# Inputs laid out by numpy in tile order, the second half of d descending, the transforms over d folded about the middle between two columns, one transfer per tile

## The chip, the cores and the metric

The kernel runs on one core of one Trainium2 chip. The metric is the device time of one execution in microseconds (us), and the number to be predicted is the median of the runs of the changed kernel. Rearranging arrays with numpy ahead of the launch, or the result behind it, is on the host and is not in that time.

## The reference

The shapes are S = 2048 tokens, D = 576 features, F = 4608 hidden units, all in 32-bit floats.

```python
xn = (x - mean(x)) / sqrt(var(x) + 1e-5)          # over D, x: [1, 2048, 576]
a  = irfft2(rfft2(xn, axes=(-2, -1)) * (w_r + 1j * w_i), s=(S, D))
b  = (sigmoid(xn @ w_gate) * (xn @ w_up)) @ w_down   # [576, 4608] twice, [4608, 576]
out = x + a + b
```

## The kernel before

**Sizes.** P = 128 partitions. The tokens make NT = 16 tiles of 128, in PAIRS = 2 pairs of 8 tiles; a pair is two chunks of CW = 512 tokens. F makes NF = 36 blocks of 128, and a block of one pair is a *unit*: 72 units in all. HD = 288 is half of D, and 288 rows are worked on as two pieces of 128 and a remainder of REM = 32. A tile of x holds the 128 tokens that leave two neighbouring remainders modulo N2 = 32, so its rows lie 32 rows apart in DRAM, and `load_x` (L340) brings it in with two transfers of 64 rows of 576 floats.

**The gated layer.** Products that need 32-bit accuracy are made of a rounded high part and a low part of each operand. ACT makes the high part with a copy, DVE the low part with a subtraction. One product (`prod`, L648) is 7 matmuls of 128x512. Units 0 and 1 of a pair are `plain` with 8 products per unit. All later ones (`unit`) use 7 products of sums and differences of the halves of xn and of the weights. The banks A, B and E of PSUM, written pA, pB and pE, collect them; between products ACT copies bank A to B, reads B into v (L712) and makes the sigmoid g (L716). `X` holds the transposed tokens with their parts: `fill` transposes x tiles on PE into px (L438, L439), ACT copies them into X (L442) and DVE makes their low part (L444). xa holds the normalised tokens, mv their moments (DVE, L351 and L352), rs their scales (L358 to L360).

**Weights.** In pair 0 every unit's weights are prepared. `load_raw` (L218, L219) brings the four 288x128 quarters of a block of w_gate and w_up into a raw tile of 128 x 4 x 3 x 128 floats: for each quarter one transfer of 2 x 128 rows, and one that puts the 32 remaining rows into the tile four times. That is 8 transfers per unit. `make_w` then makes the sums and parts (ACT L231; DVE L233, L255 to L258) and stores the result into DRAM (`wsp`, L271); the plain units do so in `make_p` (store at L262). Pair 1 reads the stored parts back (L278). w_down goes the same way: `load_d` (L285), `parts_d` (ACT L290, DVE L292), and, for the blocks whose second layer is done in 7 products, `make_t` (sums wt, then wth on ACT L312 and wtl on DVE).

**The second layer and the spectral branch.** `down` (matmuls po L755, added at L759) multiplies by w_down; in pair 1 `seven` (ps, L846, L856) does most of it. Also in pair 1 the transform runs "aside", a step between two products: `phase1b` for 16 tiles (fold of d about column 288 on DVE, transposes pf, the transform over d pd at L491, one over 64 of the tokens' indices pa at L503, stored to sc1), `phase2` for 16 steps (another transform pb L532, multiplication by w_r and w_i, L539 to L541, and back, pc L549), and `phase3` for 16 tiles (py L576, pz, the inverse over d pe L605, sums into the output tile L609 to L612, out). The fold takes e(d) = x(d) + x(576-d) and o(d) = x(d) - x(576-d) for d = 0 to 288: 289 columns, the second operand read backwards, with one padded column; so a remainder there has FR = 33 rows. KOF is the order in which the frequencies stand in the tiles: 1 to 256, 0, 257 to 288.

**What sets the order of the work.** DMA issues are mostly on SP, some at the start and the end on ACT. All engines work through their instructions in order. The kernel is written with Tile: the Python program calls the parts in turn, and a scheduler then sets each engine's order from the program's order and its own costs, except where `tc.keep_in_program_order` holds an instruction. So the diff alone does not tell the order. The program's own order at the start is this (L889 to L892):

```python
    for i in range(TPP):
        new_acc(0, i)
        if i in (TPC - 1, TPC + 1):
            load_raw(i // TPC)
```

Eight x tiles are asked for, with the raw tiles of units 0 and 1 after the fourth and the sixth of them.

## Time and profile before

| what | number |
|---|---|
| runs, us | 1441.50, 1441.35, 1441.07 |
| median, us | 1441.35 |
| span of the profiled execution, us | 1439.6 |
| DVE's costliest group, L759, 168 instructions | 126.0 us |
| DMA moved | 338.86 MB in 184747 packets, mean 235 GB/s |
| queue q1 (SP's transfers) | 72.2% of 16 engines' span |

How to read it: the profile shows one execution, whose span is 1.75 us shorter than the median of the timed runs. Each engine's busy time and number of instructions, the chain of waits and the stretches with idle time are shown where the prediction uses them. In a row of the timeline, the columns are the start in us, the length in us, the engine, its line of the program, the operation, output <- input, and the number of instructions; in brackets stands the idle time of the engine before it and what ended it. In a row of the windows stand the stretch, its length, the busy time of PE, PEld (PE's weight loads), DVE, ACT and POOL with their instruction counts, the granted TensorE clock (1.00 is full), the share of the DMA engines' time that was busy, and GB/s. A row of the groups holds line, engine, operation, shapes, count, the busy time and the mean in ns, and idle time before them.

### The profile page before, as it was taken

To read this page: it belongs to the slowest core of one execution; us is meant where nothing else is said; L and a number is where in the kernel's file an instruction comes from. 1 tells how busy PE (TensorE), PEld (TensorE's weight loads), DVE (VectorE), ACT (ScalarE), POOL (GpSimd) and SP (SyncE) were. 2 spreads that over 40 slices of the span, in tenths; PEclk is the share of its full clock that TensorE was granted. 3 is DMA by queue.
4 is the path that set the end of the run, shared out by engine and by line. 5 is a ranking of instruction groups with operands and counts; after the bars stand their busy time and mean duration, and the time that the engine had idled before them with its cause. 6 is when DMAs were issued, how large, how long until landed. Compare 5 with 4: busy or idle time off the path is not lost.

```text
span 1439.6 us, 21954 instructions
## 1 busy us (share of the span) xinstructions
PE 1425.9 (99%) x8073; PEld 1254.3 (87%) x8073; DVE 1093.5 (76%) x1798; ACT 652.3 (45%) x1122; POOL 4.8 (0%) x21
## 2 busy tenths in 40 slices
PE   8999999999999999999999999999999999999998
PEld 5888888888888888888888888888888889899997
DVE  6988788888888888756366787767888877766784
ACT  5644444444444444444345444444555534443432
POOL 0000000000000000000000000000000000000000
PEclk8999999999999999999999999999999999999999
DMA  6588788787777778664667767668998887776642
GB/s 209 207 277 294 263 295 285 254 274 258 263 261 255 262 254 277 230 231 167 226 210 203 212 197 214 196 198 275 271 275 272 267 276 246 228 224 198 204 126 83
DMA packets 184747, 338.86 MB, mean 235 GB/s; under 512 B 15808, under 2 KB 108480, under 8 KB 179776
## 3 DMA queue, kind: packets, MB, share of 16 engines
q1 hardware_dynamic: 183712, 336.15, 72.2%
q8 instruction: 64, 1.05, 0.3%
q10 hardware_dynamic: 928, 1.31, 0.3%
q14 instruction: 43, 0.35, 0.1%
HBM read 201.28 MB, written 136.12 MB: 234 GB/s over the span
## 4 chain that ended last, share of the span: by engine, by line
PE 94%; DVE 2%; DMA 1%; SPq 1%; ACT 1%; issue 1%; DVEq 0%; ACTq 0%
PE pB L648 23%; PE po L755 18%; PE pE L648 16%; PE pA L648 15%; PE ps L846 12%; PE pd L491 2%; PE pe L605 2%; PE pc L549 1%; PE py L576 1%; PE pa L503 1%; PE pb L532 1%; DMA raw<-in_B_w_up 1%; PE pf L475 1%; PE pz L588 1%; SPq L218 0%
## 5 line engine op out<-in xcount | busy, mean ns | idle before, releaser
L648 PE MATMUL pB<-X,w 128*128 128x512 f32 x1484 | 383.0, 395 | 1.9 <-ACT w L231 1.5
L648 PEld LDWEIGHTS pB<-X,w 128*128 128x128 f32 x1484 | 267.8, 188 | 51.8 <-ACT w L231 1.9
L648 PE MATMUL pE<-X,w 128*128 128x512 f32 x1064 | 272.5, 392 | 0.2 <-DVE y L713 0.2
L648 PE MATMUL pA<-X,w 128*128 128x512 f32 x1008 | 259.4, 395 | 0.3 <-DVE X L444 0.2
L648 PEld LDWEIGHTS pE<-X,w 128*128 128x128 f32 x1064 | 192.7, 188 | 34.6 <-DVE y L713 0.7
L648 PEld LDWEIGHTS pA<-X,w 128*128 128x128 f32 x1008 | 184.5, 190 | 33.9 <-DVE X L444 0.7
L755 PE MATMUL po<-wd,hh 128*128 128x288 f32 x1216 | 210.9, 295 | 0.0
L846 PE MATMUL ps<-wf,hs 128*128 128x288 f32 x1260 | 206.0, 296 | 0.3 <-issue 0.3
L846 PEld LDWEIGHTS ps<-wf,hs 128*128 128x128 f32 x1260 | 189.3, 188 | 19.4 <-DVE qs L856 1.9
L755 PEld LDWEIGHTS po<-wd,hh 128*128 128x128 f32 x1216 | 184.4, 188 | 11.2
L759 DVE TENSOR_TENSOR acc<-acc,po 128x576 f32<-128x576 f32 x168 | 126.0, 750 | 77.9 <-PE po L755 76.8
L231 ACT ACTIVATE w<-raw 128x768 fp32r<-128x768 f32 (+1 forms) x106 | 100.8, 952 | 115.6 <-PE pE L648 47.5
L755 PE MATMUL po<-wd,hl 128*128 128x288 f32 x608 | 128.9, 293 | 0.0
L856 DVE TENSOR_TENSOR qs<-qs,ps 128x576 f32<-128x576 f32 x112 | 84.1, 751 | 28.6 <-PE ps L846 27.9
L755 PEld LDWEIGHTS po<-wd,hl 128*128 128x128 f32 x608 | 98.7, 189 | 0.0
L733 DVE TENSOR_TENSOR y<-y,g 128x1024 f32<-128x1024 f32 x67 | 82.0, 1223 | 4.4 <-DVE y L732 0.5
L233 DVE TENSOR_TENSOR w<-raw,w 128x512 fp32r<-128x512 f32 (+1 forms) x106 | 82.0, 773 | 4.3 <-ACT w L231 3.3
L856 DVE TENSOR_TENSOR acc<-acc,ps 128x576 f32<-128x576 f32 x90 | 67.5, 750 | 22.9 <-PE ps L846 22.5
L716 ACT ACTIVATE g<-pB 128x512 f32<-128x512 f32 x68 | 40.7, 598 | 93.6 <-PE pB L648 93.5
L782 ACT ACTIVATE hs<-y 128x512 fp32r<-128x512 f32 x105 | 64.5, 628 | 34.3 <-DVE y L820 10.3
L732 DVE TENSOR_TENSOR y<-v,pE 128x512 f32<-128x512 f32 x67 | 45.9, 686 | 39.4 <-PE pE L648 39.3
L713 DVE TENSOR_TENSOR y<-v,pE 128x512 f32<-128x512 f32 x68 | 46.7, 687 | 33.7 <-ACT v L712 33.0
(166 smaller groups left out, 1678.8 us busy)
## 6 DMA issues: line engine op xcount, KB each, us to landing
w<-wsp SPq DMA_DIRECT2D x246, 320.0 KB
wsp<-w SPq DMA_DIRECT2D x34, 2240.0 KB
wdsp<-wd SPq DMA_DIRECT2D x36, 576.0 KB
wf<-tsp SPq DMA_DIRECT2D x60, 288.0 KB
wf<-wdsp SPq DMA_DIRECT2D x45, 288.0 KB
std<-in_B_w_down SPq DMA_DIRECT2D x36, 288.0 KB
raw<-in_B_w_gate SPq DMA_DIRECT2D x72, 128.0 KB
raw<-in_B_w_up SPq DMA_DIRECT2D x72, 128.0 KB
```

Of the source, the lines that this page charges most:

```text
L231: placed(nc.scalar.activation(o[:, :, :3, :], src, AF.Copy))
L233: placed(nc.vector.tensor_tensor(o[:, :, 3:, :], src[:, :, :KT, :], f32(o[:, :, :KT, :]), op=OP.subtract))
L648: nc.tensor.matmul(bank, w[:, sw, :], X[:, x, sx, :], start=start and j == 0, stop=stop and j == len(STEPS) - 1, skip_group_check=skip)
L713: nc.vector.tensor_tensor(y[:, 1], v[:, 1], bank["E"], op=OP.add)
L716: nc.scalar.activation(g[:, 1], bank["B"], AF.Sigmoid)
L732: nc.vector.tensor_tensor(y[:, 0], v[:, 0], bank["E"], op=OP.add)
L733: nc.vector.tensor_tensor(y, y, g, op=OP.mult)
L755: nc.tensor.matmul(pd[:, b, :HD], h[i], w[k][b], start=g == 0 and n == 0, stop=g == G - 1 and n == 2)
L759: nc.vector.tensor_tensor(a, a, pd[:, :, :HD], op=OP.add)
L782: nc.scalar.activation(hs[:, 0], src, AF.Copy)
L846: nc.tensor.matmul(pd[:, i, :HD], h[:, a, m], w[:, b], start=q == 0, stop=q == 2)
L856: nc.vector.tensor_tensor(o, o, pd[:, :, :HD], op=OP.add)
```

## The change

The host lays the inputs out in the order in which the tiles read them: x in tile order, w_gate and w_up as one array `w` with a raw tile of 128 x 1536 floats per block, the remainder rows repeated in it, w_r and w_i as one array `ri` with a tile per step of phase 2, frequencies already in the order KOF and both halves of the partitions filled. Of x, of the rows of w_gate and w_up and of the columns of w_down, the second half of d stands in descending order (COLS). The result is put back into its natural order on the host.

- A tile of x, a raw tile, a tile of ri, and an output tile of pair 0 are one transfer each; the raw tiles of units 0 and 1 are two halves. The last output tiles keep two transfers, on SP and ACT.
- The fold is about 287.5, between two columns: d with 575 - d. Its operands are the two halves as they lie, 288 columns each, none read backwards; POOL's fill of the padded column goes. The remainder of the fold has 32 rows in place of 33, and the inverse transform's matmuls (pe) write 288 columns in place of 290, as do od and the sums behind them.
- In phase 2 the two products with w_r and w_i are one instruction each over 578 columns; before they were three each (512, 2 and 64 columns).

```diff
+COLS = np.concatenate([np.arange(HD), np.arange(HD, D)[::-1]])
+ROWS = np.arange(S).reshape(N1, N2).T.ravel()
...
+    ks = np.concatenate([np.arange(KT * P), np.tile(np.arange(KT * P, HD), 4)])
+    w = np.stack([w_gate[COLS], w_up[COLS]]).reshape(2, 2, HD, NF, P)[:, :, ks]
+    w = w[[1, 1, 0, 0], [0, 1, 1, 0]].reshape(4, KT + 1, P, NF, P).transpose(3, 2, 0, 1, 4)
+    v = np.stack([w_r, w_i])[:, :, KOF].reshape(2, N1, N2 // 2, 2, KD).transpose(2, 1, 0, 3, 4)
...
     def load_raw(f):
-        cols = slice(f * P, (f + 1) * P)
         RAW[f] = raw = R["pool"].tile([P, 4, 3, P], F32, tag="raw", name=f"raw{f}", bufs=2)
-        for src, blks in ((w_gate, (3, 2)), (w_up, (0, 1))):
-            v = src.rearrange("(h r) f -> h r f", h=2)
-            for h, b in enumerate(blks):
-                nc.sync.dma_start(raw[:, b, :KT, :], v[h, :KT * P, cols].rearrange("(k p) f -> p k f", p=P))
-                nc.sync.dma_start(raw[:, b, KT, :], v[h:h + 1, KT * P:, cols].to_broadcast([4, REM, P]))
+        n = (KT + 1) * P
+        for b in ((2, 4), (0, 2)) if f < G else ((0, 4),):
+            nc.sync.dma_start(raw[:, slice(*b)].rearrange("p b k f -> p (b k f)"), w_in[f, :, b[0] * n:b[1] * n])
...
-        nc.sync.dma_start(STD[j][:, g], w_down[f * P:(f + 1) * P, :])
+        nc.sync.dma_start(STD[j][:, g], w_down[f])
...
-    def load_x(dst, t, eng=None):
-        for i, r in enumerate(rows(x, t)):
-            (eng or nc.sync).dma_start(dst[i * N1:(i + 1) * N1, :D], r)
+    def load_x(dst, t):
+        nc.sync.dma_start(dst, x[t])
...
-        xb = pool.tile([P, D + 2], F32, tag="xb", name=f"xb{t}", bufs=2)
+        xb = pool.tile([P, D], F32, tag="xb", name=f"xb{t}", bufs=2)
-        nc.gpsimd.memset(xb[:, D:], 0.0)
-            nc.vector.tensor_tensor(eo[:, e, :HD + 1], xb[:, :HD + 1], xb[:, HD:D + 1][:, ::-1], op=op)
-        rp = pool.tile([P, 2, 3, FR], F32R, tag="rp", name=f"rp{t}")
+            nc.vector.tensor_tensor(eo[:, e], xb[:, :HD], xb[:, HD:], op=op)
+        rp = pool.tile([P, 2, 3, REM], F32R, tag="rp", name=f"rp{t}")
...
-        for nm, src in (("wr", w_r), ("wi", w_i)):
-            w = pool.tile([P, 2, KD], F32, tag=nm, name=f"{nm}{i}", bufs=2)
-            v = src.rearrange("(k kl) n -> k (kl n)", kl=N2)[:, kl * KD:(kl + 2) * KD]
-            for a in range(2):
-                nc.sync.dma_start(w[a * N1:(a + 1) * N1].rearrange("p j n -> p (j n)"), v)
+        w = pool.tile([P, 2, 2, KD], F32, tag="ri", name=f"ri{i}", bufs=2)
+        nc.sync.dma_start(w.rearrange("p a j n -> p (a j n)"), ri[i])
...
-        for q, k in ((slice(0, 256), slice(1, 257)), (slice(256, 257), slice(0, 1)), (slice(257, KD), slice(257, KD))):
-            nc.vector.tensor_tensor(z[:, :, q], wr[:, :, k], pb[:, :, q], op=OP.mult)
-            nc.vector.tensor_tensor(t2[:, :, q], wi[:, :, k], sw[:, :, q], op=OP.mult)
+        nc.vector.tensor_tensor(z, wr, pb[:, :, :KD], op=OP.mult)
+        nc.vector.tensor_tensor(t2, wi, sw, op=OP.mult)
...
-                nc.tensor.matmul(pe[:, e, :NQ], l, r, start=n == 0, stop=n == len(steps) - 1)
+                nc.tensor.matmul(pe[:, e, :HD], l, r, start=n == 0, stop=n == len(steps) - 1)
-        lo, up = a[:, :HD + 1], a[:, HD + 1:][:, ::-1]
+        lo, up = a[:, :HD], a[:, HD:]
```

In the orders below a row is an engine's line, operation and tiles (output <- input) with its count; numbers at the tiles' names are buffers and differ between the two.

The first place is SP at the start, after the first requests for x. Before, SP issues this:

```order
L340 DMA acc<-in_A_x 64x576 x8
L218 DMA raw_187<-in_B_w_gate 128x2x128
L219 DMA raw_187<-in_B_w_gate 128x1x128
L218 DMA raw_187<-in_B_w_gate 128x2x128
L219 DMA raw_187<-in_B_w_gate 128x1x128
L218 DMA raw_187<-in_B_w_up 128x2x128
L219 DMA raw_187<-in_B_w_up 128x1x128
L218 DMA raw_187<-in_B_w_up 128x2x128
L219 DMA raw_187<-in_B_w_up 128x1x128
L340 DMA acc<-in_A_x 64x576 x4
```

Now SP issues this, up to the raw tiles of units 2 and 3:

```order
L344 DMA acc<-in_x 128x576 x4
L224 DMA raw_183<-in_w 128x768 x2
L344 DMA acc<-in_x 128x576 x2
L224 DMA raw_188<-in_w 128x768 x2
L344 DMA acc<-in_x 128x576 x2
L290 DMA std_501<-in_wd 128x576 x2
L276 DMA wsp_72<-w_295 128x2560
L224 DMA raw_447<-in_w 128x1536
L276 DMA wsp_73<-w_359 128x2560
L224 DMA raw_487<-in_w 128x1536
```

The last two tiles of x stand behind 10 transfers, where they stood behind 28; SP's whole list has 636 rows in place of 968. The whole raw tile of unit 2 follows the store of unit 0's parts (wsp_72) in one piece.

The second place is PE where the second 512 tokens are transposed (px_A_1, transposes of xa and of the remainder rma). Before:

```order
L648 MATMUL pE_0_479<-X,w_379 128x512 x2
L438 MATMUL px_A_1_457<-idf,xa_2_239 128x128
L439 MATMUL px_A_1_447<-idr,rma_2_2_440 96x128
L438 MATMUL px_A_1_447<-idf,xa_3_240 128x128 x2
L439 MATMUL px_A_1_447<-idr,rma_3_2_444 96x128
L438 MATMUL px_A_1_457<-idf,xa_2_239 128x128
L439 MATMUL px_A_1_457<-idr,rma_2_2_440 96x128
L438 MATMUL px_A_1_457<-idf,xa_3_240 128x128 x2
L439 MATMUL px_A_1_457<-idr,rma_3_2_444 96x128
L648 MATMUL pE_0_479<-X,w_379 128x512 x6
L648 MATMUL pA_1_525<-X,w_315 128x512 x14
```

Now:

```order
L644 MATMUL pE_0_452<-X,w_359 128x512
L442 MATMUL px_A_1_437<-idf,xa_2_219 128x128 x2
L443 MATMUL px_A_1_427<-idr,rma_2_2_420 96x128
L442 MATMUL px_A_1_427<-idf,xa_3_220 128x128 x2
L443 MATMUL px_A_1_427<-idr,rma_3_2_424 96x128
L443 MATMUL px_A_1_437<-idr,rma_2_2_420 96x128
L442 MATMUL px_A_1_437<-idf,xa_3_220 128x128 x2
L443 MATMUL px_A_1_437<-idr,rma_3_2_424 96x128
L644 MATMUL pA_1_491<-X,w_295 128x512
L644 MATMUL pE_1_492<-X,w_295 128x512
L644 MATMUL pA_1_491<-X,w_295 128x512 x13
```

The six matmuls of bank E that stood between the transposes and the first use of the new tokens (pA_1) now stand ahead of the transposes.

The third place is ACT within a unit of pair 0, where w_down's transform (wth) is made. Before:

```order
L709 ACTIVATE g_2464<-pA_2467 128x512
L312 ACTIVATE wth_2918<-wt_2865 128x1152
L712 ACTIVATE v_2465<-pB_2468 128x512
L290 ACTIVATE wd_2740<-std_2681 128x576
L290 ACTIVATE wd_2811<-std_2681 128x576
L716 ACTIVATE g_2464<-pB_2468 128x512
L231 ACTIVATE w_2655<-raw_2629 128x3x384
L699 ACTIVATE pB_2642<-pA_2641 128x512
L738 ACTIVATE hh_2627<-y_2466 128x1024
```

Now:

```order
L708 ACTIVATE v_2213<-pB_2216 128x512
L712 ACTIVATE g_2212<-pB_2216 128x512
L317 ACTIVATE wth_2790<-wt_2737 128x1152
L236 ACTIVATE w_2380<-raw_2348 128x3x384
L695 ACTIVATE pB_2354<-pA_2353 128x512
L734 ACTIVATE hh_2346<-y_2214 128x1024
L236 ACTIVATE w_2380<-raw_2348 128x2x384 x2
L702 ACTIVATE v_2351<-pB_2354 128x512
```

The transform wth has moved from between the two gates to between the second gate and the next unit's first weight part, ahead of the copy from bank A to bank B.

More of the change, by code (lines that the diff above doesn't have):

```diff
@@ L173, in spectral_glu_kernel @@
     tsp = {j: tc.dram_tile([P, 4 * 2 * HD], F32, name=f"tsp{j}") for j in SEVEN}
-    def rows(ap, t):
-        v = ap.rearrange("b (s1 s2) d -> (b s2) s1 d", s2=N2)
-        return [v[2 * t + a] for a in range(2)]
     accp = ctx.enter_context(tc.tile_pool(name="accp", bufs=1))
@@ L604, in phase3 @@
             for n, (l, r) in enumerate(steps):
[L605 to L608 removed]
+                nc.tensor.matmul(pe[:, e, :HD], l, r, start=n == 0, stop=n == len(steps) - 1)
+        od = pool.tile([P, HD], F32, tag="od", name=f"od{t}")
+        nc.scalar.activation(od, pe[:, 1, :HD], AF.Copy)
+        lo, up = a[:, :HD], a[:, HD:]
         nc.vector.tensor_tensor(lo, lo, od, op=OP.subtract)
[L610 to L612 removed]
+        nc.vector.tensor_tensor(lo, lo, pe[:, 0, :HD], op=OP.add)
+        nc.vector.tensor_tensor(up, up, od, op=OP.add)
+        nc.vector.tensor_tensor(up, up, pe[:, 0, :HD], op=OP.add)
         if t < TPP:
[L614 to L615 removed]
+            nc.sync.dma_start(out[t], a)
     def stage1():
@@ L764, in add @@
                 else:
-                    for i, r in enumerate(rows(out, t)):
-                        (nc.sync, nc.scalar)[i].dma_start(r, acc[t][i * N1:(i + 1) * N1, :])
+                    for i in range(2):
+                        (nc.sync, nc.scalar)[i].dma_start(out[t, i * N1:(i + 1) * N1], acc[t][i * N1:(i + 1) * N1, :])
         return add
@@ L965, in second_pair @@
             for m in range(TPC):
-                for k, r in enumerate(rows(x, TPP + c * TPC + m)):
-                    nc.sync.dma_start(XS[m][k * N1:(k + 1) * N1, 2 * c:2 * c + 2], r.rearrange("s (a d) -> s a d", a=2))
+                load_x(XS[m][:, 2 * c:2 * c + 2].rearrange("p a d -> p (a d)"), TPP + c * TPC + m)
         for _ in range(3):
```

72 lines of the change are left out of this document (31 added, 41 removed).

## The prediction

> **What bounds the kernel now.** I read the page first, then the windows by stage, then the timeline of the first 60 us.
>
> ```profile
> span 1439.6 us, 21954 instructions
> PE 1425.9 (99%) x8073; PEld 1254.3 (87%) x8073; DVE 1093.5 (76%) x1798; ACT 652.3 (45%) x1122; POOL 4.8 (0%) x21
> ...
> PEclk8999999999999999999999999999999999999999
> ...
> PE 94%; DVE 2%; DMA 1%; SPq 1%; ACT 1%; issue 1%; DVEq 0%; ACTq 0%
> ```
>
> PE is busy for 1425.9 of 1439.6 us and 94% of the chain is PE. All that anything but PE work can give back is the 13.7 us of PE idle, plus what a reduced clock costs. The windows (PE, PEld, DVE, ACT, POOL busy; granted clock; DMA share, GB/s) say where that lies:
>
> ```profile
> 0.00:36.00 36.00, 29.42 (x113) 20.85 (x114) 24.23 (x77) 20.19 (x41) 3.28 (x5) 0.86 0.69 209
> 36.00:72.00 36.00, 35.52 (x200) 30.03 (x199) 32.73 (x64) 23.90 (x49) 0.00 (x0) 1.00 0.56 207
> 144.00:288.00 144.00, 144.00 (x799) 127.58 (x798) 118.75 (x172) 65.09 (x86) 0.00 (x0) 1.00 0.79 274
> 1040.00:1110.00 70.00, 69.70 (x393) 61.10 (x393) 60.94 (x111) 35.38 (x60) 0.00 (x0) 1.00 0.89 276
> 1405.00:1440.00 35.00, 29.80 (x191) 27.30 (x190) 15.72 (x25) 6.47 (x12) 0.00 (x0) 0.97 0.31 86
> ```
>
> From 144 to 288 us, where most of the weight transfers run, PE has no idle time at full clock. Fewer, larger transfers are worth nothing there, although they relieve a DMA share of 0.79. Of the 13.7 us of idle, 6.6 lie in the first 36 us and 5.2 in the last 35. The change is decided at the start.
>
> ```profile
> 17.44 0.54 SPq L219 DMA_DIRECT2D raw<-in_B_w_up  x1
> 18.02 2.44 SPq L340 DMA_DIRECT2D acc<-in_A_x  x4
> ...
> 21.07 0.21 DVE L352 BATCH_NORM_AGGREGATE mv<-st 128x2 f32<-128x12 f32 x1
> 23.96 0.90 DVE L351 BATCH_NORM_STATS2 st<-acc 128x6 f32<-128x288 f32 x2 [2.68 <-DMA acc<-in_A_x]
> ...
> 26.07 0.17 DVE L358 TENSOR_SCALAR rs<-mv 128x4 f32<-128x4 f32 x1
> ...
> 26.27 0.20 ACT L360 ACTIVATE rs<-rs 128x4 f32<-128x4 f32 x1 [8.20 <-DVE rs L358]
> 26.42 0.84 ACT L231 ACTIVATE w<-raw 128x768 fp32r<-128x768 f32 x1
> ...
> 27.31 3.01 PE L648 MATMUL pB<-X,w 128*128 128x512 f32 x7 [1.50 <-ACT w L231]
> 30.71 1.12 PE L438 MATMUL px_A<-idf,xa 128*128 128x128 f32 x4 [0.38 <-ACT xa L409]
> ```
>
> Read upwards: PE waits 1.50 us for a weight part that ACT makes at 26.42; ACT does its instructions in order and stands until 26.27 for a scale from DVE; DVE stood 2.68 us for the last x tiles; and SP issued those only from 18.02 to 20.46, behind 28 other transfers. The wait is one for issue slots on SP. It has a second price, in the clock column:
>
> ```profile
> 14.90:21.70 6.80, 6.55 (x19) 4.84 (x20) 5.58 (x13) 2.88 (x6) 0.00 (x0) 0.50 0.65 166
> 25.10:28.50 3.40, 1.81 (x8) 0.87 (x7) 2.92 (x12) 2.21 (x3) 0.00 (x0) 1.00 0.58 182
> 28.50:31.90 3.40, 3.02 (x10) 2.11 (x9) 2.62 (x7) 3.39 (x8) 0.00 (x0) 0.50 0.32 88
> ```
>
> After a stretch in which PE was busy 1.81 of 3.40 us, the granted clock is 0.50 for the next 3.4 us.
>
> **The change part by part.** *SP at the start.* Before, eight x tiles take 16 issues and two weight tiles 16:
>
> ```profile
> 0.73 5.06 SPq L340 DMA_DIRECT2D acc<-in_A_x  x8
> 5.84 0.59 SPq L218 DMA_DIRECT2D raw<-in_B_w_gate  x1
> ```
>
> At 0.63 us each the last x tile is issued by 20.46. Now there are 8 + 4 issues; at 0.63 us they end at 0.73 + 12 x 0.63 = 8.3 us. Bytes then set the landing: 8 x 0.29 + 2 x 0.79 = 3.9 MB, at 209 GB/s (row 0:36) 18.8 us after the start, at 274 GB/s (row 144:288) 14.2. Either is before 21.3, where DVE is free for those tiles, so its 2.68 us vanish, and everything in the list above moves up by about 2.7. The part of w is then there at 27.26 - 2.7 = 24.6, before PE asks at 25.8 (27.31 - 1.50). **Gain 1.50 + 0.38 = 1.9 us** (bounds 1.5 and 1.9: the second wait is on xa, which stands behind the same ACT instructions).
>
> *The clock.* Without the wait at 25.8 the stretch 25.1 to 28.5 is full of matmuls and the clock should stay. 3.02 us of PE work at 0.50 would take 1.51: **gain 1.5 us** (bounds 0, if it drops all the same, and 1.5). By the Trainium skill, "TensorE: Matmul & The Clock Gate", Part 1, the clock falls only after an idle window of about 3.4 us. The row shows less is enough here: 53% busy did it. By that rule a new wait of about 1 us could never bring the slow clock back and the sum stays as it is; by the row it may, and the sum loses this 1.5.
>
> *What is late next.* With PE 3 us earlier, the copies of the second half of the tokens into X are not. Before, six pE matmuls covered them:
>
> ```profile
> 36.87 0.60 ACT L442 ACTIVATE X<-px_A 128x512 fp32r<-128x512 f32 x1 [0.90 <-PE px_A L439]
> ...
> 37.12 1.58 PE L648 MATMUL pE<-X,w 128*128 128x512 f32 x6
> 38.53 3.36 PE L648 MATMUL pA<-X,w 128*128 128x512 f32 x14
> ```
>
> In the new order no pE is left behind those transposes; pA_1 follows them directly and needs at least one copy, 0.60 us. Bounds: 0.3 (copy already running during the last transposes) and 2.0 (the 1.58 of lost cover, and a DVE half as well). I take **-0.9 us**, nearer the one copy.
>
> *First x tile.* It needs one issue instead of two:
>
> ```profile
> 4.80 0.46 DVE L351 BATCH_NORM_STATS2 st<-acc 128x6 f32<-128x288 f32 x1 [3.94 <-DMA acc<-in_A_x]
> 2.00:4.00 2.00, 1.48 (x4) 1.19 (x5) 0.00 (x0) 1.08 (x2) 1.81 (x1) 1.00 0.88 229
> ```
>
> Half an issue pair is at most 0.6 us, but the DMA engines are already 0.88 busy, so the bytes and not the issue limit most of it: **gain 0.2** (0 to 0.6).
>
> *Phase 3 matmuls* go from 290 to 288 columns, 224 of them:
>
> ```profile
> 664.10 3.18 PE po L755 x24
> 1194.37 1.87 PE pe L605 x14
> ```
>
> 133.6 ns against 132.5 ns for 288 columns: 224 x 1.1 ns = **0.25 us**, all on PE (0 to 0.45). The 96-row remainders of phase 1b have no row of their own; 99 against 96 columns of a transpose is below 0.1 us in all.
>
> *Phase 2 products.* Three column pieces become one, for two products a step:
>
> ```profile
> L539 DVE TENSOR_TENSOR z<-wr,pb x48: 150/215/691, 982.4 to 1156.2; 128x512 f32<-128x512 f32 x16, 128x2 f32<-128x2 f32 x16, 128x64 f32<-128x64 f32 x16
> ...
> L541 DVE TENSOR_TENSOR z<-z,t 128x578 f32<-128x578 f32 x16 | 12.1, 755 | 0.0
> ```
>
> 0.691 + 0.215 + 0.150 = 1.06 us becomes 0.755: 0.3 us, twice, 16 steps, 9.6 us of DVE. DVE is 60.94 of 70 busy there, but PE idles only 0.30 of those 70: **gain 0.3** (from -0.3, since the new order puts pc one or two matmuls earlier, to 1.0 over the three such stretches).
>
> *Nothing on the path:* 16 POOL memsets (nobody waits for them); the folds over d (289 reversed columns become 288 forward ones; same instructions, hidden behind PE); the output rows, whose last transfer still follows the last sum; the weight tiles after the start, covered below.
>
> Sum: 1.9 + 1.5 - 0.9 + 0.2 + 0.25 + 0.3 = 3.25 us. The profiled span goes from 1439.6 to 1436.35. The median of the runs, 1441.35, lies 1.75 above that span; with that the time is **1438.1 us**. The extremes of the terms give 1436.1 and 1442.2.
>
> **The rivals.** *DVE takes over (same).* Between 36 and 72 us DVE is busy 32.73 of 36 and PE already waits for a DVE copy there:
>
> ```profile
> 57.32 0.44 PE L438 MATMUL px_S<-idf,xa 128*128 128x128 f32 x2 [0.48 <-DVE X L444]
> ```
>
> If DVE keeps its pace while PE comes 3 us earlier, PE waits for these copies until DVE's slack (3.3 us) is used up by weight parts that the earlier raw tiles let it make first. For it: those parts now stand earlier. Against: DVE's own 2.68 us vanish too. It would leave about 1 us of the gain: 1440.3.
>
> *The first slow stretch goes as well (faster).* 14.9 to 21.7 us has 6.55 us of PE work at 0.50, 3.3 us lost. A slight shift of the start could let the clock stay up: 1438.1 - 3.3 = 1434.8. Against: the gap before it, while ACT makes the second pair of x tiles, is not touched. By the Trainium skill (same page and part) the windows run free of the program's start, which would make this a matter of luck; the three times, within 0.43 us, show no such spread.
>
> *ACT gets the longer queue (slower).* The transform of w_down (wth) now stands between the gate and the weight part, ahead of the copy into bank B, in 15 places.
>
> ```profile
> L312 ACT ACTIVATE wth<-wt 128x1152 fp32r<-128x1152 f32 x15 | 17.5, 1167 | 12.2 <-DVE wt L309 12.2
> ...
> 336.89 0.60 ACT L716 ACTIVATE g<-pB 128x512 f32<-128x512 f32 x1 [0.92 <-PE pB L648]
> 338.47 1.17 ACT L231 ACTIVATE w<-raw 128x1152 fp32r<-128x1152 f32 x1 [0.99 <-PE pE L648]
> ...
> 338.27 1.75 PE L648 MATMUL pA<-X,w 128*128 128x512 f32 x7
> ```
>
> ACT waited 0.99 us before w, so 1.17 us of wth push w to 338.65, to 339.8, and the copy (0.58) to 340.4. PE needs bank B two products of 1.59 after 338.27, at 341.45. So there is 1.05 us of slack; it decides if wt comes from DVE more than that behind the gate (DVE wt already was what wth waited for, 12.2 us in all). A mean of 0.7 us too late, 15 times, costs 10.5: 1448.6; half of it, 1443.4.
>
> *The single raw tile lands late (slower).* Now all 768 KB (128 rows of 1536 floats) stand behind the 2.29 MB store (128 rows of 4480 floats):
>
> ```profile
> 312.42 0.33 SPq L262 DMA_DIRECT2D wsp<-w  x1
> 312.80 0.49 SPq L218 DMA_DIRECT2D raw<-in_B_w_gate  x1
> ...
> 320.90 0.55 SPq L219 DMA_DIRECT2D raw<-in_B_w_up  x1
> ```
>
> 3.08 MB at 274 GB/s is 11 us, so it lands near 324; that tile is used at 338.47. It needs 14 us more to matter; each us beyond would cost up to 34 us in all.
>
> *It does not arrive earlier.* If the DMA engines and not SP held the x tiles back, the start is as it was and only 0.55 us is won: 1440.8. Against: the DMA share of the first 36 us is 0.69.
>
> **How the numbers follow.** My forecast has 0.50, DVE taking over 0.22, no earlier arrival 0.05, the first slow stretch gone 0.10, the longer ACT queue 0.10, a late raw tile 0.03. A measurement tells 0.2% from no change, 2.9 us here, so faster means under 1438.5. The forecast lies just inside; of its 0.50 I count 0.44 as faster and 0.06 as same: faster 0.54, same 0.33, slower 0.13. The range 1434.4 to 1442.8 leaves out most of the slower cases and the far end of the fastest; faster and same hold most of the chance, and the forecast's own range is 1436.1 to 1439.7.
>
> **What would show it.** Right: PE's first pB starts with no wait near 25.6 us; the granted clock is 1.00 from about 22 us on; pA_1, at 38.53 us before, starts near 36; PE has no idle from 144 to 288 us; the product on L539 shows one 128x578 form near 0.755 us. Wrong: a clock of 0.50 between 25 and 40 us, a new wait on ACT v or on X copies in every unit, PE waits on raw, or DVE waiting for x tiles after 20 us.

## The result, and the profile after

| kernel | median, us | runs | lowest to highest |
|---|---|---|---|
| before | 1441.42 | 14 | 1440.75 to 1441.60 |
| changed | 1438.87 | 14 | 1437.94 to 1439.75 |

The ratio is 0.9982, with a 95% interval of 0.9974 to 0.9990: faster by 2.55 us, clear of no change, though by 0.37 us short of the 1438.5 below which the prediction speaks of faster. The changed kernel's times lie in two groups, seven runs from 1437.94 to 1438.62 whose mean granted clock is 0.998 or more, and seven from 1439.12 to 1439.75 with 0.997, so its median depends by some tenths on how many runs fall into which. The profiled execution (1438.32 us, span 1436.5) is one of the first group; its span is 3.1 us shorter than before.

The page of the changed kernel, span, busy time and chain:

```profile
span 1436.5 us, 21196 instructions
PE 1422.8 (99%) x8073; PEld 1252.0 (87%) x8073; DVE 1087.7 (76%) x1734; ACT 653.5 (45%) x1122; POOL 3.3 (0%) x5
...
PE 97%; DVE 1%; ACT 1%; issue 0%; DMA 0%; ACTq 0%
```

PE's idle time stayed at 13.7 us (1436.5 - 1422.8; before 1439.6 - 1425.9): what got shorter is PE's own busy time, by 3.1 us. Part of that is half clock. The windows of the changed kernel (PE, PEld, DVE, ACT, POOL busy; clock; DMA share, GB/s):

```profile
14.31:17.73 3.42, 1.75 (x11) 1.20 (x11) 2.61 (x6) 3.42 (x9) 0.00 (x0) 1.00 0.20 76
17.73:21.14 3.41, 3.41 (x10) 2.63 (x9) 3.28 (x10) 0.07 (x1) 0.00 (x0) 0.50 0.44 180
...
25.10:28.50 3.40, 3.40 (x17) 2.77 (x16) 2.67 (x6) 3.39 (x7) 0.00 (x0) 1.00 0.17 64
```

Of the three stretches of 3.4 us at half clock (14.9 to 21.7 and 28.5 to 31.9) one is left, 17.7 to 21.1. The start on SP, DVE and PE, by the timeline of the changed kernel:

```profile
0.74 1.83 SPq L344 DMA_DIRECT2D acc<-in_x  x4
...
7.08 1.29 SPq L344 DMA_DIRECT2D acc<-in_x  x2
...
20.92 0.77 DVE L355 BATCH_NORM_STATS2 st<-acc 128x6 f32<-128x288 f32 x2
...
22.64 0.21 DVE L356 BATCH_NORM_AGGREGATE mv<-st 128x2 f32<-128x12 f32 x1
...
25.26 3.34 PE L644 MATMUL pB<-X,w 128*128 128x512 f32 x14
...
34.58 0.50 PE L644 MATMUL pA<-X,w 128*128 128x512 f32 x1 [0.34 <-ACT X L446]
34.92 0.39 PE L644 MATMUL pE<-X,w 128*128 128x512 f32 x1
35.69 3.24 PE L644 MATMUL pA<-X,w 128*128 128x512 f32 x13 [0.38 <-DVE X L448]
...
40.13 0.38 PE L442 MATMUL px_S<-idf,xa 128*128 128x128 f32 x2
```

The last x tiles are asked for by 8.4 us (before: 20.46), DVE takes them at 20.92 with no wait ahead (before: at 23.96 after 2.68), and pB starts at 25.26 with no wait. Two short waits for X are new. The same two marks in the kernel before:

```profile
25.82 0.21 DVE L352 BATCH_NORM_AGGREGATE mv<-st 128x2 f32<-128x12 f32 x1
...
43.33 0.38 PE L438 MATMUL px_S<-idf,xa 128*128 128x128 f32 x2
```

DVE's last moments come 3.18 us earlier and the first px_S 3.20. I call the second difference PE's **lead**: the start of a matmul before minus the start of the same matmul after. How it goes on is read from the groups kept apart by shape, whose rows hold the shortest, median and longest duration in ns and the first and last start. Before, and then after:

```profile
L476 PEld LDWEIGHTS pf<-idr,rp x32: 162/165/166, 740.0 to 947.3; 128*99 128x99 f32 x32
...
L532 PE MATMUL pb<-x2h,bmt x64: 292/296/301, 980.0 to 1153.1; 128*128 128x290 f32 x64
...
L605 PE MATMUL pe<-dit,z3h x128: 291/296/403, 1194.2 to 1411.5; 128*128 128x290 f32 x128
```

```profile
L479 PEld LDWEIGHTS pf<-idr,rp x32: 123/127/128, 736.1 to 942.6; 128*96 128x96 f32 x32
...
L530 PE MATMUL pb<-x2h,bmt x64: 294/299/311, 975.4 to 1149.9; 128*128 128x290 f32 x64
...
L602 PE MATMUL pe<-dit,z3h x128: 290/296/398, 1191.0 to 1408.3; 128*128 128x288 f32 x128
```

The lead is 3.2 us at 40 us, 3.9 at the start of phase 1b (740.0 - 736.1), 4.7 at its end, 4.6 at the start of phase 2, 3.2 at its end, and 3.2 from there to the end. So the net gain hides a loss of 1.4 us in phase 2, and gains of 0.7 between 40 and 736 us and of 0.8 in phase 1b that were not in the sum. Of the 0.7, some 0.5 comes at 86 to 96 us, where a weight load of pE stands 0.67 us for DVE's y (L713) in the kernel before and none does in the changed one; 0.2 of it is lost again by 121 us. The rest comes at 640 to 664 us and was not traced further.

### The profile page after: what moved, and what is told of

It reads as the page before. It is cut to its first block, busy times and chain, and to the rows that moved or that the text cites. A ratio compares the mean times of both kernels' runs of the same rounds, so it can differ in the third digit from the quotient of the medians.

```text
span 1436.5 us, 21196 instructions
## 1 busy us (share of the span) xinstructions
PE 1422.8 (99%) x8073; PEld 1252.0 (87%) x8073; DVE 1087.7 (76%) x1734; ACT 653.5 (45%) x1122; POOL 3.3 (0%) x5
## 3 DMA queue, kind: packets, MB, share of 16 engines
q8 instruction: 64, 1.05, 0.3%
## 4 chain that ended last, share of the span: by engine, by line
PE 97%; DVE 1%; ACT 1%; issue 0%; DMA 0%; ACTq 0%
PE pB L644 24%; PE po L751 19%; PE pE L644 16%; PE pA L644 16%; PE ps L842 12%; PE pe L602 2%; PE pd L494 2%; PE pc L546 1%; PE pa L506 1%; PE pb L530 1%; PE py L573 1%; PE pf L478 1%; PE pz L585 1%; PE b L900 0%; PE px_S L442 0%; PE px_A L442 0%
## 5 line engine op out<-in xcount | busy, mean ns | idle before, releaser
L709 DVE TENSOR_TENSOR y<-v,pE 128x512 f32<-128x512 f32 x68 | 46.7, 686 | 49.1 <-ACT v L708 48.2
L708 ACT ACTIVATE v<-pB 128x512 f32<-128x512 f32 x68 | 40.7, 598 | 71.9 <-PE pB L644 71.5
```

The costliest lines, as they stand in the source:

```text
L708: nc.scalar.activation(v[:, 1], bank["B"], AF.Copy)
L709: nc.vector.tensor_tensor(y[:, 1], v[:, 1], bank["E"], op=OP.add)
```

## The experiments

Each was run beside the kernel before on the same chip; medians of that kernel there were 1441.15 to 1441.51. Leads are read from one profiled execution of each kernel: two kernels whose phase 2 is the same but for a shift of tiles differ by 0.3 us in what they lose there, so sizes below that are not told apart.

### Is it the order of the requests alone?

```diff
     for i in range(TPP):
         new_acc(0, i)
-        if i in (TPC - 1, TPC + 1):
-            load_raw(i // TPC)
+        if i == TPC - 1:
+            load_raw(0)
+        if i == TPP - 1:
+            load_raw(1)
```

> The kernel before with one edit: the raw tile of unit 1 is asked for behind all eight x tiles. Same transfers, same bytes, same folds. Theory (the wait at the start is one for issue slots on SP): the last x tile is asked for after 24 transfers of about 0.57 us, near 14 us and not at 20.5; DVE's 2.68 us for it and PE's 1.5 us for the weight part vanish, and the slow clock behind that wait with them: 1438.0 to 1439.5. Rival 1 (size and number of the transfers, or bytes, set the start): no gain, 1441.4, or slower, as the weights of unit 1 come later. Rival 2 (the gain is in the folds, pe and phase 2): 1441.4.

1439.29 us (1439.04 to 1439.61, 11 runs) against 1441.51: 2.2 us faster, ratio 0.9984 (0.9975 to 0.9993). The timeline of that run:

```profile
10.49 4.98 SPq L340 DMA_DIRECT2D acc<-in_A_x  x8
...
21.11 0.85 DVE L351 BATCH_NORM_STATS2 st<-acc 128x6 f32<-128x288 f32 x2
...
22.93 0.21 DVE L352 BATCH_NORM_AGGREGATE mv<-st 128x2 f32<-128x12 f32 x1
...
39.86 0.38 PE L438 MATMUL px_S<-idf,xa 128*128 128x128 f32 x2
```

With not one transfer, fold or product changed, DVE's wait is gone and PE leads by 3.47 us at px_S (43.33 - 39.86). It gives back 1.1 us between 46 and 59 us and has a lead of 2.4 at phase 1b: PE stands 0.83 us at 54.95 for a copy into X that DVE makes. That unit 1's weights come later here, and DVE's work on them with them, is a likely reason, which no run tests. The theory holds, the rivals fall: most of the change's gain is to be had by putting two lines in another order. One thing else changed with them: the scheduler gave PE an order like that of the changed kernel, with the same two waits for X (0.34 and 0.38 us). The next run, which has PE's old order, shows that the gain does not come from there.

### Is it the number of the requests?

```diff
-        for b in ((2, 4), (0, 2)) if f < G else ((0, 4),):
-            nc.sync.dma_start(raw[:, slice(*b)].rearrange("p b k f -> p (b k f)"), w_in[f, :, b[0] * n:b[1] * n])
+        if f < G:
+            for b in (3, 2, 0, 1):
+                for k0, k1 in ((0, KT), (KT, KT + 1)):
+                    nc.sync.dma_start(raw[:, b, k0:k1].rearrange("p k f -> p (k f)"), w_in[f, :, b * n + k0 * P:b * n + k1 * P])
+            return
+        nc.sync.dma_start(raw.rearrange("p b k f -> p (b k f)"), w_in[f])
...
-        nc.sync.dma_start(dst, x[t])
+        for i in range(2):
+            nc.sync.dma_start(dst[i * N1:(i + 1) * N1], x[t, i * N1:(i + 1) * N1])
```

> The changed kernel, with the x tiles in two transfers each and the raw tiles of units 0 and 1 in eight each, in the order of the program; all else as changed. Theory (issue slots on SP at the start): the last x tile is asked for near 20 us again, the waits of 1.5 and 0.38 us and the slow clock after them come back: 1441 to 1442.3. Rival (folds, pe, phase 2 and the other transfers hold the gain): 1438.9.

1438.62 us (1438.47 to 1439.09, 11 runs): no slower than the changed kernel. The theory as I put it, by the count of requests, fell. The timeline shows why:

```profile
12.22 3.91 SPq L226 DMA_DIRECT2D raw<-in_w  x8
16.17 2.39 SPq L349 DMA_DIRECT2D acc<-in_x  x4
...
21.19 0.85 DVE L360 BATCH_NORM_STATS2 st<-acc 128x6 f32<-128x288 f32 x2
```

The eight requests for the second raw tile took SP 3.91 us here, where the rows lie in one piece; before they took 5.05 (12.93 to 17.98), by its timeline:

```profile
12.93 0.59 SPq L218 DMA_DIRECT2D raw<-in_B_w_gate  x1
...
17.44 0.54 SPq L219 DMA_DIRECT2D raw<-in_B_w_up  x1
```

The last x request ends at 18.56 and not 20.46, and the tile is there by 21.19, when DVE comes to it. 28 requests ahead of it cost nothing as long as it lands by about 21.2. PE has the order of the kernel before in this run, with none of the new waits for X; against that kernel DVE's last moments come 2.81 us earlier (23.01) and px_S 3.05 (40.28). So the next run cut the raw tiles into sixteen:

> The changed kernel, with the x tiles in two transfers and the raw tiles of units 0 and 1 in sixteen each. With eight pieces the last x tile was asked for by 18.6 us, DVE never waited for it, and the time was that of the changed kernel; here 44 transfers of about 0.49 us stand ahead of the last four, so these end near 22.5 us, 2 us later than in the kernel before. Theory (what counts is when the last x tile lands against the time at which DVE is free for it, about 21.2 us; neither the number of transfers nor the bytes as such): DVE waits 3 to 4 us again, PE 2 to 3 us ahead of pB: 1440.5 to 1442. Rival (the start is not worth it, and the gain is in the folds, pe and the other transfers): 1438.9.

1450.43 us (1449.94 to 1450.77, 5 runs), ratio 1.0064 (1.0050 to 1.0078). This is outside the 1440.5 to 1442 that were expected: I had sized a request at 0.49 us; these, of 64 rows, took 0.64, so the last x tile was asked for at 28.85 to 31.4, and the delay was larger than I wrote:

```profile
28.85 2.52 SPq L350 DMA_DIRECT2D acc<-in_x  x4
...
32.54 0.82 DVE L361 BATCH_NORM_STATS2 st<-acc 128x6 f32<-128x288 f32 x2 [10.68 <-DMA acc<-in_x]
...
36.23 3.36 PE L650 MATMUL pB<-X,w 128*128 128x512 f32 x7 [12.46 <-ACT w L241]
```

DVE waits of 0, 2.68 and 10.68 us go with 1438.9, 1441.4 and 1450.4 us: about one microsecond of time for each of DVE's wait. What counts is the landing of the last x tile against DVE's arrival.

### What the clock is worth, and the warm-up

PE's 21 warm-up matmuls, the *fillers*, stand ahead of the first transposes and wait for the identity idr. In the changed kernel idr lands later, as in every kernel with one transfer per x tile: 3.36 to 3.63 us in nine traces, against 2.52 to 2.60 in the five with two transfers per tile:

```profile
3.63 6.76 PE L900 MATMUL b<-idr 128*128 128x512 f32 x21 [3.63 <-DMA idr<-c_id]
10.23 0.60 PE L442 MATMUL px_A<-idf,xa 128*128 128x128 f32 x4
...
11.21 0.60 ACT L446 ACTIVATE X<-px_A 128x512 fp32r<-128x512 f32 x1 [1.50 <-PE px_A L443]
```

Before, idr was there at 2.52 and the first transposes started at 9.82. The first x tile came 0.85 us earlier (DVE starts on it at 3.95, before at 4.80), and ACT then stood 1.50 us for PE. Four of the warm-up matmuls were moved behind the first transposes:

```diff
-    todo = [(b0, ALL)] * 9 + [(b1, ALL), (b0, H0), (b1, H1), (b0, H0), (b1, H1), (b0, H0), (b1, H1), (b0, ALL),
+    todo = [(b0, ALL)] * 5 + [(b1, ALL), (b0, H0), (b1, H1), (b0, H0), (b1, H1), (b0, H0), (b1, H1), (b0, ALL),
...
-    for n in range(4):
+    for n in range(8):
         tc.keep_in_program_order(nc.tensor.matmul(b0, idr, eye, start=False, stop=True, skip_group_check=True))
```

> The changed kernel, with 4 of the 21 warm-up matmuls ahead of the first transposes moved behind them, ahead of the second ones, where PE stood idle for 1.13 us. Theory (the earlier first x tile is swallowed by the warm-up matmuls, which start later since idr lands at 3.63 and not at 2.52; and the clock falls after a stretch with too little PE work): the first transposes start near 9.1 and not at 10.23, everything up to pA moves up by about 1.0 us, and the stretch of half clock at 17.7 to 21.1 may go, worth up to 1.7: 1436.2 to 1437.9. Rival (x tiles or weights, not the warm-up, set the start): 1438.9, with more idle PE. Rival (fewer matmuls at the start bring the full clock later): slower than 1438.9, by up to 1.7.

1437.64 us (1437.01 to 1439.00, 11 runs). The first transposes start at 8.66, the last moments end 1.03 us earlier (start 21.61), px_S follows at 39.08 (1.05 earlier). The half clock did not go: it stands at 16.6 to 20.0 in this run. Five of the eleven runs took 1438.64 to 1439.00, all with a mean granted clock of 1.000, which 3.4 us of half clock would lower by 0.001; so it is no such stretch that makes these longer, and what does stays open. Then four more fillers were put ahead of the first product:

```diff
     for k in ("A11", "A12"):
         fill(0, k, 1)
+    for n in range(4):
+        tc.keep_in_program_order(nc.tensor.matmul(b0, idr, eye, start=False, stop=True, skip_group_check=True))
```

> The changed kernel with the warm-up matmuls moved as in the fourth run, and four more between the second transposes and the first product, where PE waits 0.34 us for X from ACT and 0.80 us for X from DVE. Theory (the clock halves for at least 3.4 us after a stretch of 3.4 us with too little PE work, and each such stretch costs PE up to 1.7 us): no stretch of half clock after the first 8 us, all runs in one group, at 1435.5 to 1436.6. Rival 1 (the chain over DVE and ACT, not PE, sets the pace up to 40 us, and the clock is worth little): the clock stays full, yet 1437 to 1437.6. Rival 2 (the fillers delay the first product): 1438 or more.

1437.09 us (1436.84 to 1438.92, 8 runs). The windows and the timeline of this run:

```profile
7.98:40.00 32.02, 29.71 (x152) 22.61 (x153) 26.68 (x78) 22.91 (x52) 0.00 (x0) 1.00 0.59 217
```

```profile
16.50 3.28 PE L644 MATMUL pA<-X,w 128*128 128x512 f32 x13 [0.44 <-DVE X L448]
...
23.19 0.73 PE L644 MATMUL pB<-X,w 128*128 128x512 f32 x2 [0.24 <-ACT w L236]
...
38.62 0.38 PE L442 MATMUL px_S<-idf,xa 128*128 128x128 f32 x2
```

The clock stays full from 8 us on in the profiled execution, yet px_S is only 0.46 us earlier, and PE waits for ACT again ahead of pB. Rival 1 comes nearest: up to 40 us the chain over DVE and ACT sets the pace. The expected single group did not come either: six of the eight runs took 1436.84 to 1437.44, two 1438.51 and 1438.92, again with a clock of 1.000.

The same two marks in nine profiled executions put a size on it:

| kernel | stretches of half clock, 8 to 45 us | last moments start | first px_S | difference |
|---|---|---|---|---|
| before | 14.9 to 21.7, 28.5 to 31.9 | 25.82 | 43.33 | 17.51 |
| changed | 17.7 to 21.1 | 22.64 | 40.13 | 17.49 |
| sixteen requests | 26.9 to 40.5 | 34.59 | 52.08 | 17.49 |
| eight requests | 15.8 to 22.7 | 23.01 | 40.28 | 17.27 |
| warm-up moved | 16.6 to 20.0 | 21.61 | 39.08 | 17.47 |
| remainder of 33 (below) | 15.3 to 22.1 | 23.32 | 40.92 | 17.60 |
| before, with a single product (below) | 26.7 to 33.6 | 25.87 | 44.13 | 18.26 |
| requests in another order | none | 22.93 | 39.86 | 16.93 |
| fillers ahead of pA | none | 21.75 | 38.62 | 16.87 |

In PE's new order (changed, warm-up moved, remainder of 33, and the two with none) it is 17.5 to 17.6 us from the last moments to px_S with 3.4 or 6.8 us of half clock, all of it ahead of the last moments, and 16.9 with none. So the clock is worth about 0.6 us there; the rest of a stretch at half clock is time in which PE would have waited. In the old order no execution is without half clock: it is 17.3 to 17.5 in three of them, with 6.8 to 13.7 us of it, and 18.26 in the fourth, where 6.8 us of it lie behind the last moments. What the slow stretch cost the kernel before is therefore not measured alone, and the price depends on where it lies.

### Phase 2

Phase 2 as a whole (970 to 1185 us), in the kernel before and in the changed one:

```profile
970.00:1185.00 215.00, 214.70 (x1207) 189.10 (x1206) 182.32 (x323) 106.50 (x179) 0.00 (x0) 1.00 0.88 271
```

```profile
970.00:1185.00 215.00, 214.99 (x1203) 188.07 (x1202) 175.40 (x254) 105.94 (x175) 0.00 (x0) 1.00 0.84 268
```

DVE has 6.9 us less to do and PE's idle time falls from 0.30 to 0.01 us, and yet the lead shrinks. The waits of PE's weight loads there (row: what they wait for, us in total, times, longest), before and after:

```profile
PEld pc L549 <- ACT zh L196: 3.0, 12, 0.4
```

```profile
PEld pc L546 <- ACT zh L204: 3.4, 13, 0.4
PEld pc L546 <- DVE zl L205: 1.2, 7, 0.2
```

A wait for zl, the low part that DVE makes last, is new: seven times, 1.2 us. In the new order pc's matmuls stand earlier: at one step, for example, the first of them follows one matmul of pA where it followed three. First the two products went back to three pieces:

```diff
-        nc.vector.tensor_tensor(z, wr, pb[:, :, :KD], op=OP.mult)
-        nc.vector.tensor_tensor(t2, wi, sw, op=OP.mult)
+        for q in (slice(0, 256), slice(256, 257), slice(257, KD)):
+            nc.vector.tensor_tensor(z[:, :, q], wr[:, :, q], pb[:, :, q], op=OP.mult)
+            nc.vector.tensor_tensor(t2[:, :, q], wi[:, :, q], sw[:, :, q], op=OP.mult)
```

> The changed kernel, with the two products of phase 2 in three pieces each as before (256, 1 and 32 columns of each of the two halves); all else as changed. In the traces PE's lead over the kernel before falls from 4.6 to 3.3 us over phase 2. Theory (the single piece lets pc be placed earlier, where it runs into waits): the lead stays at 4.6 and the time falls by 1.3, to 1437.6. Rival 1 (less DVE work is worth 0.3 us, and the loss has another cause, such as the new place of the tiles): 1439.2. Rival 2 (neither reaches PE): 1438.9.

1437.48 us (1437.25 to 1439.16, 7 runs). Part of the 1.4 us between the medians is how the runs fell: six of these seven took 1437.25 to 1437.90 and one 1439.16, while the changed kernel's are split evenly. The trace gives the size:

```profile
L530 PE MATMUL pb<-x2h,bmt x64: 294/298/312, 975.2 to 1149.0; 128*128 128x290 f32 x64
```

The lead goes from 4.8 to 4.1 over phase 2, a loss of 0.7 and not 1.4. The wait for zl falls to 0.3 us, and the first matmul of pc is behind three of pA again. The other direction, in the kernel before (the columns of w_r and w_i put into the order KOF by the host):

```diff
-        for q, k in ((slice(0, 256), slice(1, 257)), (slice(256, 257), slice(0, 1)), (slice(257, KD), slice(257, KD))):
-            nc.vector.tensor_tensor(z[:, :, q], wr[:, :, k], pb[:, :, q], op=OP.mult)
-            nc.vector.tensor_tensor(t2[:, :, q], wi[:, :, k], sw[:, :, q], op=OP.mult)
+        nc.vector.tensor_tensor(z, wr, pb[:, :, :KD], op=OP.mult)
+        nc.vector.tensor_tensor(t2, wi, sw, op=OP.mult)
```

> The kernel before with one edit: the host puts w_r and w_i into the order of the frequencies, and the two products of phase 2 are one instruction each. Theory (the single piece makes the scheduler place pc's matmuls earlier, where they wait for zh and zl): PE loses about 0.65 us over phase 2, 1442.0 to 1442.2. Rival 1 (less DVE work helps, as forecast: 0.3 us): 1441.1. Rival 2 (the loss in the changed kernel needs its other edits): 1441.4, no change.

1442.33 us (1442.18 to 1445.06, 11 runs) against 1441.49, ratio 1.0007 (0.9999 to 1.0016):

```profile
L532 PE MATMUL pb<-x2h,bmt x64: 292/296/301, 980.9 to 1155.0; 128*128 128x290 f32 x64
```

The lead goes from -0.9 (an earlier loss, at the start of this execution) to -1.9: one microsecond lost in phase 2 by the single product, and pc stands earlier in the same way. The interval of the ratio reaches down to no change, so the size rests on the trace. The other half of the loss does not show in the waits of weight loads, which with the three pieces are 3.2 us against 3.0 before. Is it where the one tile ri lies?

```diff
-        w = pool.tile([P, 2, 2, KD], F32, tag="ri", name=f"ri{i}", bufs=2)
+        w = pool.tile([P, 4 * KD + 16], F32, tag="ri", name=f"ri{i}", bufs=2)
+        w = w[:, :4 * KD].rearrange("p (a j n) -> p a j n", a=2, j=2)
...
```

> The third run (three pieces) with 16 unused floats more in each tile of ri, which moves the tiles behind it in SBUF. In the traces of the changed kernel and of the third run, the 80 steps from one matmul of pb to the next took 0.4 us more in all than before, with the same operands. Theory (the tile's place in SBUF, moved by the one large tile ri, slows the read by 5 ns a matmul): the 0.4 us of pb are gone, the time is 0.4 us below the third run. Rival (something else in phase 2, such as transfers or DVE at the same time): pb is as in the third run, and so is the time.

1437.65 us (1436.94 to 1439.44, 11 runs), and the lead falls from 5.2 to 4.2 in phase 2, no less than without the shift. Moving the tiles by these 16 floats does not help, and the theory fell. Then two tiles and their old transfers of 64 rows:

```diff
-        w = pool.tile([P, 2, 2, KD], F32, tag="ri", name=f"ri{i}", bufs=2)
-        nc.sync.dma_start(w.rearrange("p a j n -> p (a j n)"), ri[i])
-        wr, wi = w[:, 0], w[:, 1]
+        ws = []
+        for k, nm in enumerate(("wr", "wi")):
+            w = pool.tile([P, 2, KD], F32, tag=nm, name=f"{nm}{i}", bufs=2)
+            for a in range(2):
+                r = slice(a * N1, (a + 1) * N1)
+                nc.sync.dma_start(w[r].rearrange("p j n -> p (j n)"), ri[i, r, 2 * k * KD:(2 * k + 2) * KD])
+            ws.append(w)
+        wr, wi = ws
...
```

> The changed kernel with the three pieces of the third run, and w_r and w_i in two tiles again, with two transfers of 64 rows each. With three pieces alone PE still lost 0.65 us of its lead over phase 2, 0.4 of it between matmuls of pb. Theory (the one tile and transfer of ri, by its place or its time): the 0.4 us of pb and the 0.65 us are gone. Rival (they come from elsewhere, the new end of phase 1b or the timing of all that runs beside): both stay.

1436.85 us (1436.51 to 1438.18, 6 runs):

```profile
L535 PE MATMUL pb<-x2h,bmt x64: 292/297/301, 974.9 to 1148.0; 128*128 128x290 f32 x64
```

The lead is 5.1 at both ends: the loss is gone. So in phase 2 one tile with one transfer cost 0.7 us, and the single product the rest. Part of those 0.7 us shows in pb: from start to next start its 96 matmuls take 12.83 to 12.86 us in all in the five traces with two tiles, and 13.17 to 13.30 in the nine with one. Whether it is the one tile or its one transfer, and by what it slows PE, stays open.

### The fold's remainder

```diff
-        eo = pool.tile([P, 2, HD], F32, tag="eo", name=f"eo{t}")
+        eo = pool.tile([P, 2, HD + 2], F32, tag="eo", name=f"eo{t}")
+        nc.gpsimd.memset(eo[:, :, HD:], 0.0)
...
-        rp = pool.tile([P, 2, 3, REM], F32R, tag="rp", name=f"rp{t}")
+        rp = pool.tile([P, 2, 3, FR], F32R, tag="rp", name=f"rp{t}")
...
-            steps.append((fr[:KR, e, :], cf[:KR, e, 4, :]))
+            steps.append((fr[:3 * FR, e, :], cf[:3 * FR, e, 4, :]))
```

> The changed kernel with one zero column more in each half of the fold of phase 1b, so that the remainder has 33 columns again and its transposes load 99 columns as weights, not 96 (165 against 127 ns in the two traces). Theory (PE's lead gained 0.75 us over phase 1b because these 32 weight loads are 38 ns shorter and the next transposes start sooner): the lead is lost again, 0.4 to 0.8 us, and the transposes behind them start later by about 30 ns each. Rival (the gain there is from the folds on DVE, whose second operand is no longer read backwards, or from fewer transfers): no change in the lead over phase 1b.

1438.86 us (1438.36 to 1440.06, 11 runs): by the times alone no difference from 1438.87. In the trace the weight loads are back at 165 ns and the lead grows by 0.4 us over phase 1b (736.9 to 943.8 against 740.0 to 947.3, so 3.1 to 3.5), where it grew by 0.8 in the changed kernel. So about half of the gain there is the three columns less in these loads; where the other half comes from stays open. The size is of one trace: in the nine other kernels with 96 columns the lead grows by 0.6 to 0.85 us over phase 1b, in the two others with 99 and the old fold by nothing.

### All repairs together

The fillers with the three pieces, and then with the two tiles as well:

> The changed kernel with the fillers of the sixth run and the three pieces of phase 2 of the third. If the two gains lie in different places and add up, it is 0.65 us below the sixth run (PE's lead lost over phase 2 went from 1.35 to 0.7 us with the pieces). If the pieces' gain was only the luck of the clock at the start, it equals the sixth run.

1436.21 us (1436.11 to 1436.91, 5 runs), against 1437.09 without the pieces; 0.88 less; of the two sizes that the expectation gave, 0.65 and nothing, it is nearer the first. In the traces phase 2 costs 0.6 us of lead in place of 1.4.

> The changed kernel with the fillers of the sixth run, the three pieces of phase 2, and w_r and w_i in two tiles with two transfers each. If the three repairs lie in different places and add up: 0.65 us below the seventh run (1436.2), 1435.3 to 1435.8, with a clock that stays full after the first 8 us in most runs. If the return to the old transfers in the tenth run only looked better by the luck of the clock at the start: 1436.2.

1435.93 us (1435.66 to 1437.32, 5 runs), ratio to the kernel before 0.9964 (0.9951 to 0.9978). Its page and its first px_S:

```profile
span 1434.1 us, 21353 instructions
...
PE 1421.2 (99%) x8077; PEld 1251.4 (87%) x8077; DVE 1090.7 (76%) x1798; ACT 652.0 (45%) x1122; POOL 3.3 (0%) x5
```

```profile
38.91 0.38 PE L442 MATMUL px_S<-idf,xa 128*128 128x128 f32 x2
...
L535 PE MATMUL pb<-x2h,bmt x64: 292/296/302, 974.3 to 1147.4; 128*128 128x290 f32 x64
```

Phase 2 costs no lead here either (5.7 at both ends). The time misses the 1435.3 to 1435.8 expected by 0.13 us: the step from the run before is 0.3 us and not 0.65. In the profiled execution the start was 0.3 us slower (px_S at 38.91, there at 38.60); if that holds for the other runs, it makes up the difference. This version beats both kernels: 5.2 us below the kernel before and 2.9 below the changed one.

## Why the prediction was right, point by point

Forecast 1438.1 us, from 1434.4 to 1442.8, and a span of 1436.35; measured 1438.87 and 1436.5. The mechanism at the start is the one forecast; that the total fits this well is luck, since errors of both signs met behind it. At the start 3.2 us were gained and 2.7 forecast; later 0.7 came before phase 1b and 0.8 in it, where nothing was forecast, and 1.4 were lost in phase 2, where 0.3 was to be gained. Two small slips in the working change nothing: the best ends of the terms add up to 5.15 us, which gives 1436.2 and not 1436.1, and the last window reaches 0.4 us past the end, so PE is idle for 4.8 us there and not 5.2.

- **What bounds the kernel, and where the change is decided:** right. From 144 to 288 us PE was and is busy for 144.00 us; the larger transfers are worth nothing there.
- **The wait for issue slots on SP** (1.9 us): the cause is right and shown by the run that only reorders the requests, by the one with eight requests, in which PE keeps its old order, and by the three sizes of DVE's wait. The number of requests was the wrong measure: with as many as before, but faster ones, the loss did not come back.
- **The clock** (1.5 us, as a term of its own beside the wait): the slow stretch went, as forecast, but this term was no separate gain. The chain over DVE and ACT moved by 3.18 us, PE followed it by 3.20, and clearing what half clock is left in the changed kernel is worth about 0.6. The sum for the start, 1.9 + 1.5 - 0.9 + 0.2 = 2.7, came out near 3.2 for a simpler reason: DVE's 2.68 us, plus about half a microsecond by which DVE finished the work ahead of it and the tiles themselves earlier. The rival "DVE takes over" had the right mechanism for this stage, that DVE sets PE's pace, and the wrong price, since DVE itself came 3.2 us earlier. Behind 40 us, where it placed the waits, the changed kernel loses nothing; the run that only reorders the requests does, 1.1 us.
- **The copies into X, late next** (-0.9 us, bounds 0.3 and 2.0): 0.34 + 0.38 = 0.72 us of new waits. In the run with eight requests the scheduler kept the old order, these waits are not there, and from the last moments to px_S it is 17.27 us and not 17.49. So the waits are real, but by this pair some 0.2 us of them was a price, the rest time in which PE would have waited elsewhere; as the two differ in their half clock too (6.8 and 3.4 us), that size is not shown.
- **The first x tile** (+0.2): it came 0.85 us earlier and was swallowed by the warm-up matmuls, which started later. Moving four of them gave 1.0 us.
- **Phase 2** (+0.3, bounds -0.3 and 1.0): wrong in sign and outside its bounds, 1.4 us lost. The step that failed is the bound: it took the 0.30 us that PE idles in 70 for all that there is to gain or lose, and it gave the one tile ri no term. One half of the loss is the single product: pc's weight loads wait up to 0.4 us each, 4.6 us in all in place of 3.0, and such a wait need not show as idle PE. The other half is the one tile with its one transfer, by a way that stays open.
- **Phase 1b** (below 0.1): 0.8 gained, about half of it by the 32 weight loads of 96 columns in place of 99, 38 ns shorter each.
- **Phase 3** (+0.25): the term is right and yet does not reach the time. From start to next start the 224 matmuls of pe take 30.20 us in all before and 29.96 in the changed kernel, 0.24 less; but the lead is 3.2 at both ends, so something else in phase 3 takes as much, which was not looked for.
- **Rivals:** no wait in ACT's longer queue and none for the raw tiles: PE is never idle from 72 to 720 us in the changed kernel's windows, and its lead stays at 3.5 to 3.6 us from 113 to 640. Of the first slow stretch half went, without the 3.3 us that I had priced for all of it.

## What to carry to other kernels

A request that stands behind others on an issuing queue can cost as much as a slow transfer: before laying data out anew, look at when the last consumer is free, and whether the order of requests alone gets its tile there in time. A half clock costs only where PE sets the pace; measure from the last event of the chain that feeds it, not by the length of the slow stretch. And PE that is "never idle" can still lose time: weight loads that wait in pieces of up to 0.4 us, which an innocent merging of instructions elsewhere brought about here through the scheduler. So compare the start of the same matmul in both traces, stage by stage.

## What the runs showed of the hardware

The granted clock changed at distances of 3.41 us or multiples of it (before: 14.86, 21.69, 28.52, 31.93). Laid out in such steps, it fell after stretches in which PE was busy 1.72 us (before, 11.45 to 14.86), 1.75 (changed, 14.31 to 17.73), 1.81 (before, 25.1 to 28.5) and 1.88 (two tiles and old transfers, 13.22 to 16.63), and stayed after 1.90 and 2.08 (requests in another order, 11.42 to 14.84 and 14.84 to 18.25) and 2.25 (changed, 10.90 to 14.31). None of these stretches was idle as a whole. One stretch of each kind, of the kernel before and of the run with the other order:

```profile
11.45:14.86 3.41, 1.72 (x10) 0.97 (x9) 2.20 (x7) 3.41 (x9) 0.00 (x0) 1.00 0.80 220
```

```profile
11.42:14.84 3.42, 1.90 (x11) 1.15 (x9) 2.19 (x9) 3.42 (x9) 0.00 (x0) 1.00 0.77 214
```

So in these runs the limit lay near 55% of PE busy, as the profile counts it. The Trainium skill, "TensorE: Matmul & The Clock Gate", Part 1, names one idle window of about 3.4 us as what brings the slow clock; the length agrees, but these rows show that a window idle for a little under half is enough.

A weight load of 99 columns took 165 ns and one of 96 took 127, 30% more for 3% more columns. And eight requests for the same 768 KB took SP 4.58 and 5.05 us in the kernel before, where the rows of 128 floats lay apart, and 3.90 and 3.91 in the run with eight requests, where they lay together.
